# A gated attention unit followed by an FFT-convolution gate: output stores on three queues, a third tile between relu and square, and a planner that models two transfer queues

## The chip, the cores and the metric

The kernel runs on one core of one Trainium2 chip. The metric is the device time of one execution in microseconds, the median of several runs.

## The reference

Eight batches of 3136 rows. For each batch an attention without softmax (relu, then square), gated by `u`, and then a long convolution by FFT between two gates:

```python
scores = (1 / S) * z @ z.T                     # S = 3136, z is S x 64
x = u * (np.maximum(scores, 0) ** 2 @ v)       # u, v are S x 256
proj = x @ w_proj                              # 256 -> 3 * 256
x1, x2, x3 = proj[..., :D], proj[..., D:2*D], proj[..., 2*D:]
x2_conv = irfft(rfft(x2, axis=1) * rfft(filter_fft, axis=0), n=S, axis=1)
out = (x1 * x2_conv * x3) @ w_out              # float32, 8 x 3136 x 256
```

## The kernel before

The rows of a batch are cut into seven chunks of columns (`CHUNKS`: five of 512, one of 256, one of 320) and 25 tiles of 128 rows. For each chunk PE forms score tiles (`score_mm`, transposed, in the three pairs of PSUM banks `ps_s`). ACT applies relu into a tile `R`, ACT or DVE squares it into a tile `A` (`relu` L1819, `sq` L1826 and L1828), and PE multiplies by `v` (`weigh`, PSUM tiles `ps_o`). The scores are symmetric, so tiles for later chunks are transposed by DMA into `M1`, `M2e` and `M2o` instead of being computed twice (`mirror`, L1752). A score group of 64 contracted rows can also be issued as four 64x64 quadrants instead of two halves, which spares a change of PE's tiling next to transform work (the branch on `plan.mode`).

When a chunk of `x` is complete (`xT`, L1871), `add_proj` multiplies it by `w_proj`: the gates `x1 * x3` (`gate_t`, L1214) and the first stage of a two-stage transform (`dft1`, PE matmul `x_t,T`, tile `s_t`), which is stored to a DRAM scratch `spec_0` or `spec_1` (L1018). After all chunks `add_spectrum` loads this back in another layout (`load_spec`, L1048, four loads of three DMAs into `spec_in_t`), does the second stage on PE in 64x64 quadrants (`S`, tiles `xh` or `R`), multiplies by the filter's spectrum `H` (L1302), inverts it (`TZ`, tile `gs_t` and others) and stores it to scratch (L1347). `add_end` loads that by chunk (`load_c`, L1060, `conv_in_t`), does the last inverse stage (`T,conv_in_t`), multiplies by the gate (`yT_t`, L1388), multiplies by `w_out` (`wo,yT_t`), copies to a tile (`ost_t`) and stores it in `out` (L1447), two DMAs a chunk, one for each half of the partitions.

SP issues all plain transfers and DMA transposes, in one queue. POOL issues the loads that cast to 16 bit (`v_t`, `un_t`, `zn_t`, L649 and L668); each group of them waits for a `tick` (L658). In the last batch (b = 7) other tiles are free, so the spectrum's loads use `M_t` and `M2e_t` too, its stores come from `gs_t`, `M2o_t`, `A_t` and `uT_t`, and the loads of the inverse go to seven tiles `A_t`. Four chunks of batch 6 are held back (`HOLD = 3`, kind `FZ`) as work for the waits of the last batch; their results lie in `v_t` and `ost_t`. The last batch's own chunks end in the order of `FINAL`, with results in `R_t`, `xh` and `gs_t`.

The order of all of this is decided when the program is built. Every step is a `Task` with a cost on its engine, what it depends on and which buffers it takes. `Plan.go` replays the engines with these costs and emits the steps in the order in which it starts them. A step that moves data (`moves`) takes a place on a transfer bus: `moves` us after the one before it, no sooner than `DMA_GO` after its issue, landed `DMA_DONE` (and `late`) after that. Which kind of work PE takes next is a weighted sum over the plan's state (`pick_pe`); there are eight sets of weights, `a` to `h`, and the string `MIX` names one for every 12 steps. On the chip each engine follows this order, and semaphores hold it where the data are late.

Of the kernel before, what the change touches and what calls it, by code (L numbers as in the profile page):

```python
# [11 lines left out]
P = 128  # L12
F32 = mybir.dt.float32
BF16 = mybir.dt.bfloat16
# [4 lines left out]
N1 = 64  # L19
# [10 lines left out]
LATE_OUT = 2.0  # L30
AFTER = (1, 3, 5, 6)
# [7 lines left out]
class Weights:  # L39
# [82 lines left out]
    "chbeegbghbaageecebgfecfgbadeeedffbcgebdcgbececaahhfbceddhcdegbdhdhegdefcehbcagec"  # L122
    "abbbdgfdgbdhchhdchcaedhfhhaeacbaadeebfaaabfccdgdffdfaacccfebchccdabdfbdbeeccafae"
    "fhchhgabfghcchhgdfgdeggaaaa"
# [23 lines left out]
DMA_GO, DMA_DONE = 1.2, 0.8  # L148
# [121 lines left out]
class Plan:  # L270


    def __init__(self):
# [9 lines left out]
        self.bus = 0.0  # L283
# [31 lines left out]
    def run(self, task, engine, start):  # L315
# [130 lines left out]
def kernel(  # L446
# [57 lines left out]
    R_p = Pool("R", 2, [P, 2, 512], F32)  # L504
    A_p = Pool("A", 8, [P, 1024], BF16)
# [245 lines left out]
    filt_ld = [Task(lambda e, x=x: load_filter(*x), {"POOL": 1.6}, lat=10.0) for x in filt_cuts]  # L751
# [252 lines left out]
    def dft1(kind, get, t0, nt, dst, deps, free=None, late=0.0):  # L1004
# [20 lines left out]
        c = on("SP", put, 0.4, [b_], moves=0.35 * nt, late=late)  # L1025
# [16 lines left out]
    def load_spec(src, j0, nj, deps, late=0.0, home=l_p):  # L1042
# [7 lines left out]
        t = on("SP", go, 1.3, [*deps, *((d, ISSUED) for d in loads[-1:])], [home.slots], moves=0.6 * nj, late=late)  # L1050
        return in_order(t), box

    def load_c(src, c, deps, home):
# [8 lines left out]
        if home is c_p:  # L1062
            return in_order(on("SP", go, 0.45, [*deps, *((d, ISSUED) for d in loads[-1:])], [home.slots], moves=0.4 * nt, late=LATE_C)), box
        return on("SP", go, 0.45, deps, [home.slots], moves=0.4 * nt), box
# [203 lines left out]
    def add_spectrum(b, puts):  # L1268
# [9 lines left out]
        for g in range(NJ // 2):  # L1278
# [35 lines left out]
            def inv(g=g, xb=xb, z_=z_, a0=a0, gh=gh, mine=mine, per=per):  # L1314
# [29 lines left out]

                def put():
                    for rows, part in by_row(D2[b % 2], gx["g"], 2 * j0, 2 * per):
                        nc.sync.dma_start(out=rows, in_=part)  # L1347

                p_ = on("SP", put, 1.2, gx["es"], moves=0.5 * per, late=LATE_D2 * (not final))
# [10 lines left out]
    def add_end(b, lasts, gtasks, cs, kind="FB", src=c_p, dsts=(o_p,), late=0, behind=(), then=(), split=False, mids=(y_p,)):  # L1360
        for at, c in enumerate(cs):
# [82 lines left out]
            def store(i0, n, c=c, ob=ob):  # L1444
                r = rows_n1(out[b])
                for j, lo, hi, n2 in runs(T0[c] + i0, T0[c] + i0 + n):
                    nc.sync.dma_start(  # L1447
                        out=r[:, n2 : n2 + hi - lo, :], in_=ob["o"][ds(j * N1, N1), i0 : i0 + hi - lo, :]
                    )
# [515 lines left out]
```

## Time and profile before

| | us |
|---|---|
| timed runs | 992.66, 985.16, 992.11 |
| median | 992.11 |
| profiled execution | 981.7 |
| its span, first to last instruction | 979.9 |
| PE, ACT, DVE, POOL busy in the span | 940.6, 872.4, 827.4, 186.2 |
| DMA: moved in the span | 170.26 MB, mean 174 GB/s |

The profiled execution took 981.7 us, 10.4 less than the median of the timed runs. In rows of groups the columns are line, engine, operation, output from input with shapes, count, busy us, mean ns of one, and the idle time before them with what ended it. SPq is SP's instruction queue, in which DMAs are issued; the length of such a row is that of the issue, not of the transfer. Line numbers are those of the kernel before; in the rows of order of the changed kernel they are some 5 to 24 higher for the same statement.

### The profile page before, as it was taken

What the parts mean: (1) busy time and instruction counts of PE and PEld (TensorE: products, weight loads), DVE (VectorE), ACT (ScalarE), POOL (GpSimd) and SP (SyncE); (2) the same over time, 40 slices, a digit from 0 to 9 for tenths busy, and PEclk for the clock granted to TensorE, in tenths of its full rate; (3) what the DMA queues carried; (4) which work ended last, traced back from release to release, by engine and by line L of the source; (5) the groups of instructions that cost most, each with busy time, mean ns of one, the idle gap of its engine ahead of it and who ended that gap; (6) DMA issues with size and microseconds to landing.
All of it is one profiled execution on the core that took longest, in us unless ns stands there. A gap on an engine that the chain in (4) does not pass through costs nothing.

```text
span 979.9 us, 18879 instructions
## 1 busy us (share of the span) xinstructions
PE 940.6 (96%) x6450; PEld 468.4 (48%) x6560; DVE 827.4 (84%) x1449; ACT 872.4 (89%) x1203; POOL 186.2 (19%) x403
## 2 busy tenths in 40 slices
PE   6999999999999999999999999999999999999975
PEld 2343644355544554446544454445554365444644
DVE  7966788988889888888889978899889988799775
ACT  5996899999889899999989999899889999999774
POOL 5142311222021302113111320131102130001000
PEclk9999999999999999999999999999999999999989
DMA  9899688977999798998799878999699987995668
GB/s 163 139 165 174 115 175 165 180 141 138 188 208 199 155 184 168 189 184 154 152 222 194 170 151 169 206 175 178 145 191 213 185 149 168 199 179 129 170 175 244
DMA packets 332371, 170.26 MB, mean 174 GB/s; under 512 B 242442, under 2 KB 307786, under 8 KB 332276
## 3 DMA queue, kind: packets, MB, share of 16 engines
q1 hardware_dynamic: 304548, 138.10, 65.3%
q0 software_dynamic: 27728, 30.97, 23.6%
q8 instruction: 51, 0.84, 0.4%
q14 instruction: 44, 0.36, 0.1%
HBM read 90.26 MB, written 53.35 MB: 147 GB/s over the span
## 4 chain that ended last, share of the span: by engine, by line
PE 88%; DMA 4%; DVE 3%; ACT 2%; issue 1%; SPq 1%; ACTq 0%; DVEq 0%
PE ps_o_t L575 52%; PE ps_s L575 36%; DVE A_t L1828 1%; DMA spec_in_t<-spec 1%; DMA ost_t<-in_z_dram 1%; ACT R_t L1819 1%; DMA spec<-gs_t 1%; SPq L700 1%; DMA conv_in_t<-spec 1%; DMA spec<-s_t 0%; DMA A_t<-spec 0%; DVE yT_t L1388 0%; ACT xh L608 0%; ACT gs_t L608 0%; SPq L1447 0%
## 5 line engine op out<-in xcount | busy, mean ns | idle before, releaser
L1819 ACT ACTIVATE R_t<-ps_s 128x1024 f32<-128x1024 f32 (+4 forms) x512 | 473.7, 957 | 53.6 <-PE ps_s L575 39.3
L575 PE MATMUL ps_o_t<-A_t,v_t 128*128 128x512 bf16 (+3 forms) x1998 | 465.0, 354 | 8.0 <-issue 3.5
L1828 DVE TENSOR_TENSOR A_t<-R_t 128x1024 bf16<-128x1024 f32 (+3 forms) x312 | 346.1, 1128 | 77.6 <-ACT R_t L1819 76.9
L575 PEld LDWEIGHTS <-v_t 128*128 128x128 bf16 (+2 forms) x2846 | 249.8, 98 | 271.1 <-issue 88.4
L1826 ACT ACTIVATE A_t<-R_t 128x1024 bf16<-128x1024 f32 (+4 forms) x184 | 181.2, 990 | 2.1
L575 PE MATMUL ps_s<-zT_t 64*128 64x512 bf16 (+4 forms) x1246 | 152.5, 355 | 3.3 <-DVE s_t L612 2.0
L658 POOL COPY tick<-xT_t 1x1 bf16<-1x1 bf16 x54 | 11.7, 216 | 684.7 <-DVE xT_t L1871 669.4
L575 PE MATMUL ps_s<-xT_t,wp 128*128 128x512 bf16 (+2 forms) x392 | 105.0, 352 | 1.0 <-DVE gate_t L1214 0.4
L608 ACT ACTIVATE x_t<-ps_s 128x512 bf16<-128x512 f32 (+2 forms) x143 | 78.6, 565 | 10.7 <-PE ps_s L575 8.0
L1871 DVE SCALAR_TENSOR_TENSOR xT_t<-ps_o_t,uT_t 128x256 bf16<-128x256 f32 (+2 forms) x224 | 76.0, 380 | 13.3 <-PE ps_o_t L575 11.4
L575 PEld LDWEIGHTS <-zT_t 64*128 64x128 bf16 (+1 forms) x1279 | 49.9, 98 | 77.7 <-issue 60.1
L575 PE MATMUL ps_o_t<-M_t,v_t 128*128 128x512 bf16 (+2 forms) x352 | 81.9, 353 | 0.4
L1302 DVE TENSOR_TENSOR xh<-xh,H 128x1024 bf16<-128x1024 bf16 x120 | 81.3, 682 | 1.2 <-ACT xh L608 0.2
L1214 DVE TENSOR_TENSOR gate_t<-ps_s,x_t 128x256 bf16<-128x256 f32 (+2 forms) x214 | 72.8, 383 | 8.9 <-PE ps_s L575 5.3
L1388 DVE TENSOR_TENSOR yT_t<-ps_s,gate_t 128x512 bf16<-128x512 f32 (+2 forms) x99 | 59.3, 617 | 5.2 <-PE ps_s L575 3.7
L649 POOL DMA_DIRECT2D un_t<-in_u_dram x112 | 59.9, 556 | 9.4 <-issue 3.6
L668 POOL DMA_DIRECT2D v_t<-in_v_dram x112 | 59.5, 556 | 7.1 <-issue 3.1
L575 PE MATMUL ps_s<-wp,xT_t 128*128 128x256 bf16 x398 | 58.4, 273 | 0.2
L575 PEld LDWEIGHTS <-wp 128*128 128x128 bf16 x448 | 41.6, 98 | 34.4 <-issue 6.5
L608 ACT ACTIVATE xh<-ps_s 128x512 bf16<-128x512 f32 (+1 forms) x86 | 48.3, 607 | 8.8 <-PE ps_s L575 8.5
L575 PE MATMUL ps_s<-wo,yT_t 128*128 128x256 bf16 (+1 forms) x356 | 54.0, 273 | 0.4 <-DVE yT_t L1388 0.3
L608 ACT ACTIVATE s_t<-ps_s 128x512 bf16<-128x512 f32 x80 | 47.0, 592 | 2.3 <-PE ps_s L575 1.8
(149 smaller groups left out, 823.0 us busy)
## 6 DMA issues: line engine op xcount, KB each, us to landing
out_dram<-ost_t SPq DMA_DIRECT2D x66, 256.0 KB
spec<-s_t SPq DMA_DIRECT2D x96, 128.0 KB
spec_in_t<-spec SPq DMA_DIRECT2D x60, 192.0 KB
spec<-gs_t SPq DMA_DIRECT2D x60, 192.0 KB
v_t<-in_v_dram POOLq DMA_DIRECT2D x80, 128.0 KB, 5.0
un_t<-in_u_dram POOLq DMA_DIRECT2D x80, 128.0 KB, 5.2
conv_in_t<-spec SPq DMA_DIRECT2D x33, 256.0 KB
out_dram<-ost_t SPq DMA_DIRECT2D x19, 128.0 KB
```

Source lines behind the costliest of these rows:

```text
L575: wrote(nc.tensor.matmul(o, *args, **kw), o)
L608: got = nc.scalar.activation(out_, in_, AF.Copy)
L649: nc.gpsimd.dma_start(out=t[ds(j * N1, N1), lo - t0 : hi - t0, :], in_=x[:, n2 : n2 + hi - lo, :])
L658: nc.gpsimd.tensor_copy(tick[:], xt["t"][0:1, 1, 0:1])
L668: nc.gpsimd.dma_start(out=t[ds(j * N1, N1), ds(v_at(a), (b - a) * D)], in_=r[:, n2 + a - lo : n2 + b - lo, :].rearrange("p t d -> p (t d)"),)
L1214: got = nc.vector.tensor_tensor(g[:, ::-1] if h == 0 else g, p, x, ALU.mult)
L1302: nc.vector.tensor_tensor(x[:, 1 - i], x[:, 0], h, ALU.mult)
L1388: got = nc.vector.tensor_tensor(yb["y"][:, dh, 0:w], p, gates[b, c, dh][:, 0:w], ALU.mult)
L1819: has_read(nc.scalar.activation(blocks(box["R"], n, cw)[:rows], p, AF.Relu), p)
L1826: nc.scalar.activation(a, r, AF.Square)
L1828: nc.vector.tensor_tensor(a, r, r, ALU.mult)
L1871: nc.vector.scalar_tensor_tensor(x, f, inv_s2, ut, ALU.mult, ALU.mult)
```

## The change

1. *Stores.* In `add_end` a store names its queue. The last batch's chunks are stored half by SP and half by POOL, the last two of them half by SP and half by ACT; the last chunk's parts as before by pairs of tiles, of which it has one. The held chunks of batch 6 (kind `FZ`) are stored by POOL, both halves. In `add_spectrum` of the last batch the store of the last set but one (from `A_t`) goes to POOL. The stores of the second and third chunk of batch 6 that are not held have to be issued after the last first-stage store of the last batch (`put_off_stores`, joined with `puts[-1]`).
2. *Tiles.* `R` has three tiles instead of two, `A` seven instead of eight.
3. *The planner.* The bus becomes two, one for POOL and one for the others; when both are in use, each slows the other. The casting loads take a place on POOL's (0.515 us a tile) where they had a fixed 8 or 10 us. `DMA_GO` and `DMA_DONE` go from 1.2 and 0.8 to 0.9 and 0.6. The transfers' costs are set anew, those of the plain ones lower, those of the transposes mostly higher.
4. *The order.* `MIX` is another string of the same length; all weights stay.

```diff
-DMA_GO, DMA_DONE = 1.2, 0.8
+DMA_GO, DMA_DONE = 0.9, 0.6
...
-        self.bus = 0.0
+        self.bus = [0.0, 22.0]
...
         if task.moves:
-            self.bus = max(end + DMA_GO, self.bus) + task.moves
-            lat = self.bus + DMA_DONE + task.late - end
+            mine = int(engine == "POOL")
+            first = max(end + DMA_GO, self.bus[mine])
+            both = min(task.moves, max(0.0, self.bus[1 - mine] - first))
+            self.bus[mine] = first + task.moves + both
+            self.bus[1 - mine] += both
+            lat = self.bus[mine] + DMA_DONE + task.late - end
...
-    R_p = Pool("R", 2, [P, 2, 512], F32)
-    A_p = Pool("A", 8, [P, 1024], BF16)
+    R_p = Pool("R", 3, [P, 2, 512], F32)
+    A_p = Pool("A", 7, [P, 1024], BF16)
...
-        t = on("SP", go, 1.3, [*deps, *((d, ISSUED) for d in loads[-1:])], [home.slots], moves=0.6 * nj, late=late)
+        t = on("SP", go, 1.3, [*deps, *((d, ISSUED) for d in loads[-1:])], [home.slots], moves=0.37 * nj, late=late)
...
+                aside = final and mine == sets[-2]
...
-                        nc.sync.dma_start(out=rows, in_=part)
+                        (nc.gpsimd if aside else nc.sync).dma_start(out=rows, in_=part)
...
-            if split and c == cs[-1]:
-                for k, e_ in enumerate(oe):
-                    s_ = on("SP", lambda i0=2 * k, n=min(2, nt - 2 * k), store=store: store(i0, n), 0.9, [e_, *behind], prio=1, moves=0.9)
+            if split:
+                second = "ACT" if at >= len(cs) - 2 else "POOL"
+                parts = [(2 * k, min(2, nt - 2 * k), [e_]) for k, e_ in enumerate(oe)] if c == cs[-1] else [(0, nt, oe)]
+                todo = [
+                    (e, x, y, half, made_, 0.45 * y / 2) for x, y, made_ in parts for half, e in enumerate(("SP", second))
+                    if any(r_[0] == half for r_ in runs(T0[c] + x, T0[c] + x + y))
+                ]
             else:
-                s_ = on("SP", lambda nt=nt, store=store: store(0, nt), 1.3, [*oe, *behind], prio=1, moves=0.45 * nt, late=LATE_OUT * (dst is o_p))
-            s_.frees.append((o0, 1))
+                todo = [("POOL" if kind == "FZ" else "SP", 0, nt, None, oe, 0.45 * nt)]
...
+            if b == B - 2 and kind == "FB" and at:
+                put_off_stores.append(s_)
...
-                cu[slots[x]] = on("POOL", lambda: cast_u(*slots[x]), 1.1, [tick_], [un_p.slots], lat=8.0)
+                cu[slots[x]] = on("POOL", lambda: cast_u(*slots[x]), 1.1, [tick_], [un_p.slots], moves=CAST * len(tiles[slots[x][1]]), late=LATE_CAST)
...
+                        for t in put_off_stores:
+                            join(t, puts[-1], ISSUED)
```

How this moves instructions is shown at three places, each first as it was and then as it is.

DVE between the last cast of a first-stage tile `s_t` of the last batch and the first eviction of its spectrum, `xh_120`. In it `yT_t` is a product of the inverse with a gate (chunks of batch 6), `gate_t` a product of the last batch's projections. Before:

```order
L612 CAST s_t<-ps_s_139 128x256
L1214 TENSOR_TENSOR gate_t<-ps_o_t,x_t 128x4x64 x2
L1388 TENSOR_TENSOR yT_t<-ps_s_141,gate_t 128x512
L1388 TENSOR_TENSOR yT_t<-ps_s_139,gate_t 128x512
L1388 TENSOR_TENSOR yT_t<-ps_o_t,gate_t 128x512
L1214 TENSOR_TENSOR gate_t<-ps_s_141,x_t 128x4x64 x4
L1388 TENSOR_TENSOR yT_t<-ps_o_t,gate_t 128x512
L612 CAST xh_120<-ps_s_140 128x512
```

And after the change, the same stretch:

```order
L617 CAST s_t<-ps_s_139 128x256
L1395 TENSOR_TENSOR yT_t<-ps_s_140,gate_t 128x512
L1395 TENSOR_TENSOR yT_t<-ps_o_t,gate_t 128x512
L1219 TENSOR_TENSOR gate_t<-ps_s_140,x_t 128x4x64 x2
L1219 TENSOR_TENSOR gate_t<-ps_s_139,x_t 128x4x64 x2
L617 CAST xh_120<-ps_s_141 128x512
```

Two `yT_t` and two gate products have left this stretch; they stand behind the last multiplication by `H` now.

SP from the last stores of the last batch's spectrum to the loads of its inverse; `out_dram<-v_t` are stores of held chunks of batch 6. Before:

```order
L1347 DMA spec_1_62<-M2o_t 2x2048
L1347 DMA spec_1_62<-A_t 48x1024 x2
L1347 DMA spec_1_62<-A_t 2x1024
L1347 DMA spec_1_62<-uT_t 48x1024 x2
L1347 DMA spec_1_62<-uT_t 2x1024
L1447 DMA out_dram<-v_t 64x1024 x2
L1447 DMA out_dram<-v_t 64x512 x2
L1060 DMA A_t<-spec_1_62 128x4x256 x3
```

And now, where `ost_t` is a chunk of batch 6 that is not held:

```order
L1354 DMA spec_1_62<-M2o_t 2x2048
L1456 DMA out_dram<-ost_t 64x1024 x2
L1354 DMA spec_1_62<-uT_t 48x1024 x2
L1354 DMA spec_1_62<-uT_t 2x1024
L1065 DMA A_t<-spec_1_62 128x4x256 x3
```

The store from `A_t` and those of the held chunks have gone to POOL, and an output store stands ahead of the one from `uT_t`.

The end of SP's queue, the stores of the last batch's chunks. Before, both halves of each:

```order
L1447 DMA out_dram<-R_t 64x1024 x2
L1447 DMA out_dram<-xh_118 64x1024 x2
L1447 DMA out_dram<-gs_t 64x1024 x2
L1447 DMA out_dram<-R_t 64x768
L1447 DMA out_dram<-R_t 64x512
L1447 DMA out_dram<-xh_119 64x1024 x2
L1447 DMA out_dram<-gs_t 64x1024 x2
L1447 DMA out_dram<-xh_120 64x512 x2
```

After the change, SP's end:

```order
L1456 DMA out_dram<-R_t 64x1024
L1456 DMA out_dram<-xh_118 64x1024
L1456 DMA out_dram<-gs_t 64x1024
L1456 DMA out_dram<-xh_119 64x1024
L1456 DMA out_dram<-R_t 64x768
L1456 DMA out_dram<-gs_t 64x1024
L1456 DMA out_dram<-xh_120 64x512
```

And ACT's end, with its last three copies:

```order
L613 ACTIVATE R_t<-ps_o_t 128x512
L613 ACTIVATE R_t<-ps_o_t 64x256
L613 ACTIVATE xh_120<-ps_s_140 128x512
L1456 DMA out_dram<-gs_t 64x1024
L1456 DMA out_dram<-xh_120 64x512
```

Of each chunk one half has left SP; those of the last two chunks stand on ACT behind its last copy, the other five on POOL.

More of the change, by code (lines that the diff above doesn't have):

```diff
@@ L750 @@
     filt_cuts = ((0, 8), (8, 16), (16, NT))
[L751 removed]
+    filt_ld = [Task(lambda e, x=x: load_filter(*x), {"POOL": 1.6}, moves=CAST * (x[1] - x[0]), late=LATE_CAST) for x in filt_cuts]
     for x in filt_ld:
@@ L1555, in go_v @@
                     cv.setdefault(n, []).append(
-                        on("POOL", gv, 0.3 * (hi - lo), [tick_], [v_p.slots] if first else [], lat=8.0)
+                        on("POOL", gv, 0.3 * (hi - lo), [tick_], [v_p.slots] if first else [], moves=CAST * (hi - lo), late=LATE_CAST)
                     )
```

43 lines of the change are left out of this document (27 added, 16 removed).

## The prediction

> **What bounds the kernel now.** I read the page first, then the windows by stage, then the list of waits on PE, the chain of waits at the end, and the timeline of SP's queue there. The page, first span and busy time, then the chain and the groups used as prices:
>
> ```profile
> span 979.9 us, 18879 instructions
> PE 940.6 (96%) x6450; PEld 468.4 (48%) x6560; DVE 827.4 (84%) x1449; ACT 872.4 (89%) x1203; POOL 186.2 (19%) x403
> ...
> PE 88%; DMA 4%; DVE 3%; ACT 2%; issue 1%; SPq 1%; ACTq 0%; DVEq 0%
> ...
> L575 PE MATMUL ps_o_t<-A_t,v_t 128*128 128x512 bf16 (+3 forms) x1998 | 465.0, 354 | 8.0 <-issue 3.5
> ...
> L575 PE MATMUL ps_s<-wo,yT_t 128*128 128x256 bf16 (+1 forms) x356 | 54.0, 273 | 0.4 <-DVE yT_t L1388 0.3
> L575 PE MATMUL ps_s<-T,conv_in_t 128*128 128x128 bf16 (+1 forms) x324 | 30.5, 218 | 0.1
> ```
>
> TensorE is busy for 940.6 of 979.9 us, so only 39.3 us of the span are open to any change of order. Busy time over count gives prices: 465.0/1998 = 0.233 us for a 512-wide matmul, 54.0/356 = 0.152 for one of the output projection, 30.5/324 = 0.094 for one of the inverse transform. The windows say where the 39.3 us lie (busy time of PE, PEld, DVE, ACT, POOL, then clock, DMA share and GB/s):
>
> ```profile
> 0.00:14.00 14.00, 6.36 (x31) 2.43 (x31) 8.66 (x42) 6.56 (x10) 10.68 (x30) 1.00 0.86 169
> 14.00:75.00 61.00, 57.96 (x312) 24.06 (x318) 50.48 (x83) 54.22 (x67) 16.30 (x33) 1.00 0.98 152
> 75.00:82.00 7.00, 5.03 (x18) 1.49 (x14) 3.29 (x4) 3.25 (x4) 0.52 (x1) 0.76 1.33 132
> 82.00:925.60 843.60, 834.39 (x5713) 416.60 (x5814) 728.49 (x1247) 776.83 (x1064) 158.71 (x340) 1.00 0.90 174
> 925.60:934.30 8.70, 4.65 (x37) 2.71 (x35) 5.28 (x13) 3.31 (x6) 0.00 (x0) 1.00 0.55 146
> 934.30:950.10 15.80, 13.65 (x177) 8.15 (x180) 14.34 (x24) 13.62 (x28) 0.00 (x0) 0.78 0.59 162
> 950.10:971.90 21.80, 18.62 (x175) 12.93 (x175) 16.92 (x40) 14.64 (x29) 0.00 (x0) 1.00 0.84 248
> 971.90:979.90 8.00, 0.00 (x0) 0.00 (x0) 0.00 (x0) 0.01 (x1) 0.00 (x0) 0.72 0.64 210
> ```
>
> In the 843.6 us of the middle PE is busy for 834.4 (99%): nothing can be won there, only lost. The losses are 7.6 us in the first 14 (the first load, which the change leaves alone), 2 us at 75 to 82 with the clock at 0.76, and everything after 925.6: a wait of four us, a stretch of 21.8 us with PE at 18.62, and 8.0 us after the last copy in which no engine computes. PE's own waits, longest first:
>
> ```profile
> PE ps_s L578 <- ACT xT_t L608: 5.3, 1, 5.3
> PE ps_s L575 <- DMA spec_in_t<-spec: 5.0, 2, 4.1
> PE ps_o_t L575 <- issue: 3.5, 22, 0.2
> PE ps_s L575 <- DVE s_t L612: 2.0, 1, 2.0
> ```
>
> The spectrum's loads cost PE 5.0 us in two waits: 4.1 in the last batch, 0.9 in one earlier one. SP's queue at the end (start, length, what):
>
> ```profile
> 949.13 2.20 SPq L1347 DMA_DIRECT2D spec<-M2o_t  x3
> 951.44 1.80 SPq L1347 DMA_DIRECT2D spec<-A_t  x3
> 953.36 1.34 SPq L1347 DMA_DIRECT2D spec<-uT_t  x3
> 954.79 2.86 SPq L1447 DMA_DIRECT2D out_dram<-v_t  x4
> 957.76 4.23 SPq L1060 DMA_DIRECT2D A_t<-spec  x7
> ...
> 969.76 1.87 SPq L1447 DMA_DIRECT2D out_dram<-R_t  x2
> 971.72 1.20 SPq L1447 DMA_DIRECT2D out_dram<-xh  x2
> 973.02 1.86 SPq L1447 DMA_DIRECT2D out_dram<-gs_t  x2
> 974.97 1.78 SPq L1447 DMA_DIRECT2D out_dram<-xh  x2
> ```
>
> SP issues for 4.8 us after the last copy has ended (976.75 against 971.9), and the last bytes land 3.1 us later, at 979.9.
>
> **The change, part by part.** The sum is made against the profiled execution's own 981.7 us (span 979.9). The median of the three timed runs is 992.11, 10.4 us above; I carry the difference over to it.
>
> *Stores after the last copy.* Each chunk's store is now one half on SP and one on POOL (the last two chunks: on ACT). At 0.6 to 0.9 us a half (rows 971.72 to 974.97, two to a row) SP has one issue left after the last copy. ACT has two, since its half of the last chunk but one stands behind its own last copy; no issue on ACT is in the trace, so I price it by SP's rows, 1.2 to 1.8 for two, and take 1.5. Nothing else waits behind them. With 3.1 us to land that is 4.6 in place of 8.0, a gain of 3.4. The bounds: if nothing but the rate counts, 285 GB/s was moved while PE ended its work and 210 afterwards:
>
> ```profile
> 961.44:971.90 10.46, 9.30 (x100) 7.35 (x100) 8.00 (x15) 6.97 (x13) 0.00 (x0) 1.00 0.93 285
> ```
>
> That is 10.46 x 285 + 8.0 x 210 = 4.66 MB, or 16.4 us at 285 GB/s, which ends at 977.8: a gain of 2.1. Issue time alone gives 3.7 at most. I take the 3.4, because in the last stretch (next part) the data come later and so more slowly. The Trainium skill ("DMA: Bandwidth & Descriptors", section "Issuing engines are not separate DMA queues") says that transfers issued from several engines share the same 16 DMA engines, so that only issue time is saved; by it this part would be the 2.1 and not the 3.4. The trace leaves that open: a DMA share of 0.93 speaks for the rule, 0.64 after 971.9 against it.
>
> *Work moved behind the last spectrum.* The order rows of DVE show four yT products and six gate products between the last s_t cast and the first xh before, two and four now. On PE, 36 matmuls stood between the last first-stage transform and the first use of the spectrum, 16 now: four 512-wide, eight of the output and eight of the inverse fewer, 4 x 0.233 + 8 x 0.152 + 8 x 0.094 = 2.9 us of the 4.65 that covered the wait. The wait grows from 4.1 to about 7.0. That alone delays nothing: the chain through the transfers,
>
> ```profile
> 926.23 4.17 DMA spec<-s_t
> ...
> 931.30 2.98 DMA spec_in_t<-spec
> ...
> 957.76 3.63 DMA A_t<-spec
> ```
>
> keeps its length, since its stores stand in SP's queue as before, ahead of two of the four output stores that used to precede them. But the work comes back in the last stretch. After its last quadrant of the inverse, PE has eight more 512-wide, eight more output and twelve more inverse matmuls there: 8 x 0.233 + 8 x 0.152 + 12 x 0.094 = 4.2 us. DVE, after its last multiplication by H, has four more gate products, three more yT products and one more copy; by
>
> ```profile
> 955.21 1.62 DVE L1214 TENSOR_TENSOR gate_t<-ps_s,x_t 128x256 bf16<-128x256 f32 x4 [0.44 <-PE ps_s L575]
> 951.30 0.68 DVE L1388 TENSOR_TENSOR yT_t<-ps_o_t,gate_t 128x512 bf16<-128x512 f32 x1
> 950.70 0.69 DVE L612 CAST uT_t<-ps_s 128x512 bf16<-128x512 f32 x1
> ```
>
> that is 1.62 + 3 x 0.68 + 0.69 = 4.4 us. PE then needs 18.62 + 4.2 = 22.8 us in a stretch of 21.8, DVE 16.92 + 4.4 = 21.3. So the last copy comes at least 1.0 later; with the idle 3.2 us of before less the 0.7 that PE waited for A_t, 3.5 later. I take 2.2, midway.
>
> *The held stores and one spectrum store to POOL.* SP loses the 1.80 of spec<-A_t and the 2.86 of out_dram<-v_t ahead of the A_t loads. These can start up to 1.9 us sooner, but PE has work for that time now (above), so I cost it at nothing; without that cover it is worth the 0.7. POOL has nothing else to do after 925.6 (0.00 busy), so nobody waits behind these issues; a POOL issue costs about 0.56, as in the casts.
>
> *Third R tile, seven A tiles.* ACT's relu no longer waits for the square two before it; in the middle PE is at 99%, so this hides behind PE: nothing, and the lost A tile the same.
>
> *New order, new transfer costs.* PE's work is the same, but for 156 half-size score matmuls that became 78 whole ones. It changes its tiling 607 times instead of 601; the gaps at such a place are
>
> ```profile
> 883.44 0.05 issue
> ...
> 908.68 0.16 issue
> ```
>
> so six more cost 0.3 to 1.0, I take 0.6. Between the last first-stage transform of a batch and the first use of its spectrum stood at least 89 matmuls before; now 76 and 82 in batches 3 and 4. The planner counts shorter transfers, so I allow one more wait of the earlier kind, 0.9 (5.0 - 4.1); below it nothing, above it one in each of the seven earlier batches and at as many loads behind them, about 8. In the head one transpose held SP for 6.94 us against a median of 1.26 (minimum, median, maximum in ns):
>
> ```profile
> L1752 SPq DMA_TRANSPOSE M_t<-A_t x96: 1159/1260/6937, 16.6 to 908.7; - x96
> ```
>
> It ended in PE's wait of 2.0 for s_t, then half a clock for some 3.5 us. The rows around it stand otherwise now, and 95 of 96 such transposes were shorter, so I count the 2.0 as won; between 0 (it comes again) and 3.7 (the clock too).
>
> Sum: -3.4 + 2.2 + 0.6 + 0.9 - 2.0 = -1.7 us: 981.7 becomes 980.0, and on the median 992.11 becomes 990.4.
>
> **Rivals.** *The transfers take it back, no gain at the end.* If the stores after the last copy are bound by rate, they start later by the 2.2 and gain only 2.1: the end gives +0.1. With the stall of the head coming again and 1.5 in the middle the time is 993.7. For it speaks the DMA share of 0.93 in the stretch that now holds more work; against it the falling rate after 971.9.
>
> *Slower: the planner's shorter transfers.* With first uses set closer to their loads, PE stands still in the middle. Place: the first use of the spectrum and of its second to fourth loads. Price: 0.9 to 4.1 a wait (the two seen). From two waits of 2.5 (midway) it outweighs all gains; with four, and the stall of the head in its place, the time is 992.11 - 3.4 + 2.2 + 0.6 + 10 = 1001.5. For it: 76 and 82 against 89. Against it: batch 0 and 2 had 91 and 89 before, and no wait.
>
> *Faster: the order hides more.* The head gains 3.7, the last stretch grows by 1.0 only, six tilings cost 0.3, and the 9.2 us of idle between 82 and 925.6 shrink by half: -3.4 + 1.0 + 0.3 - 3.7 - 4.6 = -10.4, or 981.7. For it: the third R tile and transfers counted where the casts run. Against it: most of these 9.2 us are short gaps of issue.
>
> *The change doesn't do what it says* (issues wait on POOL or ACT as on SP) falls together with the first rival.
>
> **How the numbers follow.** A measurement of this kernel can tell about 1% from no change (the three runs lie 0.8% apart). The forecast (-6 to +1, so 986 to 993) has 0.42, no gain 0.22, slower 0.20, faster 0.16. Faster by over 1% is the last alone, 0.16; within 1% the first two, 0.64; slower 0.20. The range holds the forecast, the case of no gain and about half of each of the others: down to 978, which is the faster case less half of the 0.8% that the runs lie apart, and up to 1001, the slower case; what lies beyond is about 0.1 on the slow side and 0.05 on the fast one.
>
> **What would show it.** Right: after the last copy 4 to 5 us, not 8; two engines' stores side by side; the wait for spec_in_t near 7 and the last stretch 23 to 25 us; DVE and PE there above 90%. Wrong: 7 us or more after the last copy (first rival), waits of PE for spec_in_t or conv_in_t in batches 3 and 4 (second), or a transpose of some 7 us again near 75. A middle whose idle time is under 5 us would make the forecast too slow.

## The result, and the profile after

| | before | after |
|---|---|---|
| median, us (20 runs each, one disturbed run of 1097.75 after left out of the comparison) | 987.68 | 986.82 |
| lowest and highest of the others | 979.83 to 992.66 | 984.07 to 990.87 |
| ratio after/before, 95% interval | | 0.9998 [0.9977, 1.0018] |
| profiled execution, its span | 981.7, 979.9 | 984.44, 982.7 |

The change makes no difference that these runs can tell. The median of before over 20 runs is 4.4 us below the 992.11 of the three runs shown first, and its profiled execution is among its shortest. So the two profiles differ by more (+2.8 us in span) than the medians (-0.9), and single stages are compared below over several runs.

The page of after, first its span and PE, then the chain that ended last:

```profile
span 982.7 us, 18875 instructions
...
PE 950.0 (97%) x6484; PEld 467.6 (48%) x6484; DVE 809.5 (82%) x1426; ACT 873.3 (89%) x1226; POOL 199.3 (20%) x419
...
PE 89%; DMA 5%; DVE 2%; SPq 1%; ACT 1%; issue 1%; DVEq 0%; ACTq 0%
```

PE shows 9.4 us more than before. Most of that is no new work: before, the trace has 6560 weight loads and 6450 matmuls, so some 110 matmul records are missing; now both are 6484. Idle time of PE that was read from the profile before is therefore too long in places. The windows of after, cut at the same events as those of before (last cast of `s_t`, first use of the spectrum, last quadrant of the inverse, last copy), with the same columns:

```profile
82.00:925.44 843.44, 839.82 (x5726) 415.25 (x5725) 709.93 (x1219) 776.13 (x1086) 163.05 (x339) 1.00 0.89 174
925.44:932.35 6.91, 1.71 (x9) 0.59 (x7) 2.61 (x6) 1.20 (x3) 0.00 (x0) 0.83 0.84 230
932.35:948.55 16.20, 14.80 (x185) 7.50 (x186) 13.48 (x23) 13.58 (x28) 0.00 (x0) 0.75 0.41 107
948.55:974.16 25.61, 21.49 (x192) 14.93 (x192) 19.96 (x47) 16.54 (x32) 8.57 (x16) 1.00 0.89 260
974.16:982.67 8.51, 0.00 (x0) 0.00 (x0) 0.00 (x0) 0.00 (x0) 0.00 (x0) 0.72 0.44 138
```

To set beside these, the same events of before to 0.01 us are 926.66, 934.32, 950.60, 971.91 and the end 979.90. The last `s_t` is 1.2 sooner, the wait for the spectrum 0.75 shorter (6.91 against 7.66), the last stretch 4.3 longer (25.61 against 21.31), and the time behind the last copy is not shorter: 8.51 against 7.99. PE's waits of after, longest first:

```profile
PE ps_s L580 <- DMA spec_in_t<-spec: 6.6, 2, 5.2
PE ps_s L583 <- ACT xT_t L613: 5.5, 1, 5.5
PE ps_s L580 <- DMA A_t<-spec: 2.3, 2, 1.6
...
PE ps_s L580 <- DVE s_t L617: 1.1, 1, 1.1
```

The wait for the last spectrum is 5.2; all others for `spec_in_t` are 1.4 together (6.6 - 5.2). The waits for `A_t<-spec` are 2.3, where there was one of 0.7 before.

What ended the program stands in POOL's queue. The rows of its drain, an instruction that the program has at its end on each engine, of after and then of before (minimum, median and maximum in ns, first and last start):

```profile
L1984 POOLq DRAIN  x3: 46/102/8721, 973.2 to 982.4; - x3
```

```profile
L1960 POOLq DRAIN  x3: 45/102/7487, 904.0 to 979.6; - x3
```

Before, POOL's last issue was at 904.0, and its drain of 7.49 us was over at 911.5. After the change POOL issues its last half store at 973.19, the drain starts there and takes 8.72 us, to 981.88; 0.8 later the program ends. SP reaches its own drain rows when its last transfers have landed:

```profile
L1984 SPq DRAIN  x3: 7/7/13, 979.6 to 982.1; - x3
```

That is at 979.6, 2.3 us before POOL's drain is over; in before SP was there at 979.1, 0.8 before the end. The windows say the same: no byte starts to move in the last 3.8 us of after (0 GB/s from 978.90 to 982.67), against 1.5 us in before (978.40 to 979.90). The ends of SP's queue and of POOL's, in after:

```profile
973.42 0.47 SPq L1456 DMA_DIRECT2D out_dram<-R_t  x1
973.98 0.55 SPq L1456 DMA_DIRECT2D out_dram<-gs_t  x1
974.62 1.21 SPq L1456 DMA_DIRECT2D out_dram<-xh  x1
```

```profile
971.33 0.54 POOL L1456 DMA_DIRECT2D out_dram<-xh  x1 [1.79 <-ACT xh L613]
973.19 0.54 POOL L1456 DMA_DIRECT2D out_dram<-R_t  x1 [1.32 <-ACT R_t L613]
```

SP is done with its issues 1.7 us after the last copy (975.83 against 974.16; before 4.85), so the split did at SP what was forecast. The transfer itself isn't what the drain lasts for: POOL's last store had landed 3.7 us after its issue, near 976.9, by the list of DMA issues:

```profile
out_dram<-R_t POOLq DMA_DIRECT2D x1, 128.0 KB, 3.7
```

### The profile page after: what moved, and what is told of

Its sections match the earlier page's. It is cut to its first block, busy times and chain, and to the rows that moved or that the text cites. A ratio compares the mean times of both kernels' runs of the same rounds, so it can differ in the third digit from the quotient of the medians.

```text
span 982.7 us, 18875 instructions
## 1 busy us (share of the span) xinstructions
PE 950.0 (97%) x6484; PEld 467.6 (48%) x6484; DVE 809.5 (82%) x1426; ACT 873.3 (89%) x1226; POOL 199.3 (20%) x419
## 4 chain that ended last, share of the span: by engine, by line
PE 89%; DMA 5%; DVE 2%; SPq 1%; ACT 1%; issue 1%; DVEq 0%; ACTq 0%
PE ps_o_t L580 53%; PE ps_s L580 36%; DMA M_t<-A_t 2%; DMA spec_in_t<-spec 1%; DMA A_t<-spec 1%; DMA M2e_t<-A_t 1%; DMA ost_t<-in_z_dram 1%; DVE A_t L1850 1%; SPq L705 1%; ACT x_t L613 0%; SPq L1053 0%; DMA spec<-uT_t 0%; DVE R_t L1307 0%; DVE uT_t L1395 0%; DVE xT_t L617 0%
## 5 line engine op out<-in xcount | busy, mean ns | idle before, releaser
L1841 ACT ACTIVATE R_t<-ps_s 128x1024 f32<-128x1024 f32 (+4 forms) x512 | 463.8, 967 | 47.8 <-PE ps_s L580 43.7
L580 PE MATMUL ps_o_t<-A_t,v_t 128*128 128x512 bf16 (+4 forms) x2074 | 475.9, 355 | 1.7 <-DVE A_t L1850 1.6
L1850 DVE TENSOR_TENSOR A_t<-R_t 128x1024 bf16<-128x1024 f32 (+3 forms) x306 | 338.9, 1125 | 80.1 <-ACT R_t L1841 72.3
L1848 ACT ACTIVATE A_t<-R_t 128x1024 bf16<-128x1024 f32 (+4 forms) x190 | 190.5, 1010 | 3.6 <-DMA M_t<-A_t 2.3
L663 POOL COPY tick<-xT_t 1x1 bf16<-1x1 bf16 x54 | 16.0, 296 | 679.8 <-DVE xT_t L1893 679.8
L580 PE MATMUL ps_s<-zT_t 64*128 64x512 bf16 (+4 forms) x1168 | 149.5, 356 | 1.0 <-DVE zT_t L617 0.5
L580 PE MATMUL ps_s<-xT_t,wp 128*128 128x512 bf16 (+2 forms) x434 | 112.3, 352 | 1.4 <-DVE s_t L617 1.1
L613 ACT ACTIVATE x_t<-ps_s 128x512 bf16<-128x512 f32 (+2 forms) x149 | 82.1, 579 | 13.0 <-PE ps_s L580 11.1
L613 ACT ACTIVATE s_t<-ps_s 128x512 bf16<-128x512 f32 (+1 forms) x83 | 48.7, 602 | 7.3 <-PE ps_s L580 5.7
L580 PE MATMUL ps_s<-wo,yT_t 128*128 128x256 bf16 (+1 forms) x340 | 51.4, 273 | 0.0
```

The source lines that it names most:

```text
L580: wrote(nc.tensor.matmul(o, *args, **kw), o)
L613: got = nc.scalar.activation(out_, in_, AF.Copy)
L663: nc.gpsimd.tensor_copy(tick[:], xt["t"][0:1, 1, 0:1])
L1841: has_read(nc.scalar.activation(blocks(box["R"], n, cw)[:rows], p, AF.Relu), p)
L1848: nc.scalar.activation(a, r, AF.Square)
L1850: nc.vector.tensor_tensor(a, r, r, ALU.mult)
```

## The experiments

Three theories of the time behind the last copy: *issue* (the one on record: SP's queue sets it), *rate* (the first rival: the bytes left and what 16 DMA engines move), and *drain* (formed from the profile of after: POOL's drain sets it, if POOL issues late). For the last stretch, from the last quadrant of the inverse to the last copy: the moved work alone, or the held stores that now run beside the loads of `A_t`. Ratios are to the kernel before in the same call, with 95% intervals. All kernels keep the order that their planner gave; only the queue or the place of an issue is edited, except in `before_r3`. Stages are read from one profile of each kernel.

**halves_act.** After, with POOL's halves of the last batch on ACT.

```diff
-                queue = {"SP": nc.sync, "ACT": nc.scalar, "POOL": nc.gpsimd}[e]
+                queue = {"SP": nc.sync, "ACT": nc.scalar, "POOL": nc.scalar if b == B - 1 else nc.gpsimd}[e]
```

> The changed kernel, but the five half stores of the last batch that went to POOL are issued by ACT; the planner still counts them as POOL's, so the order on PE, DVE and SP is the same. Drain theory: the end of the program waits for POOL's drain, which lasts until about 8 us after POOL's last DMA issue (8.7 us from 973.2 in the changed kernel, 7.5 us from 904.0 in the one before). POOL's last issue is then the one of the held chunk near 959, so the drain is over long before, and the end is set by the last landing on SP and ACT: the span falls from 982.7 to about 980.5, and POOL's long drain ends near 967. Rate theory: the last stores are bound by how fast the bytes move, whichever queue issues them: the span stays at 982.7 within 0.5. Cost that both allow: five issues of 0.5 us on ACT among its copies, up to 1 us.

984.56 us, 0.9975 [0.9948, 1.0002]. POOL's drain was over at 972.95, the program ended at 986.28, 6.55 us after the last copy. But the last copy came 51.3 us after the last `s_t`, 2.6 later than in after. I first took this for ACT's issues, four of which (0.56, 0.51, 0.50, 0.50) now lie among its copies, and the expectation of `order_act2` below says so. PE's waits behind 945 show another reason for a part of it:

```profile
PE ps_s L580 <- DMA A_t<-spec: 3.3, 3, 1.9
PE ps_o_t L580 <- ACT x_t L613: 0.4, 1, 0.4
```

PE waited 3.3 us for the loads of `A_t` here (2.3 in after), and in `both`, below, the same seven issues on ACT delay nothing that can be seen. This explains 1.0 of the 2.6; the rest stays open, and the profile of this kernel (988.12) is long beside its median.

**held_behind.** After, with the held stores on SP behind the last load of `A_t`.

```diff
+                last_loads.append(c)
+                if len(last_loads) == NC:
+                    loads_out.append(True)
+                    for x in waiting_stores:
+                        x()
...
-                queue = {"SP": nc.sync, "ACT": nc.scalar, "POOL": nc.gpsimd}[e]
+                if kind == "FZ" and not loads_out:
+                    waiting_stores.append(lambda: store(e, i0, n, half, c, ob))
+                    return
+                queue = {"SP": nc.sync, "ACT": nc.scalar, "POOL": nc.sync if kind == "FZ" else nc.gpsimd}[e]
```

> The changed kernel, but the held chunks' stores of batch 6 go to SP, behind the seven loads of A_t, instead of to POOL beside them. Contention theory: these 1.8 MB moved side by side with the loads and stretched the first one from 3.6 to 7.4 us; without them the loads land by about 959.5 instead of 962.5, PE's waits of 2.3 us for A_t go, and the last copy comes about 2 us sooner, near 972; since POOL's last issue moves with it, the span falls to about 980.7. Rival, the cover theory: PE, ACT and DVE have work until 962 anyway, so the last copy moves by less than 0.7 us and the span stays between 982 and 983.5.

984.06 us, 0.9980 [0.9958, 1.0001]. From the last quadrant of the inverse to the last copy 23.54 us, 2.1 less than in after. In the waits of PE behind 925 none for `A_t` is left:

```profile
PE ps_s L580 <- DMA spec_in_t<-spec: 5.1, 1, 5.1
PE ps_s L580 <- ACT xh L613: 0.6, 1, 0.6
PE ps_o_t L580 <- DVE yT_t L1402: 0.6, 1, 0.6
```

So about half of the 4.3 by which the stretch grew goes with the wait for `A_t`, and comes from held stores that move before the loads are through. (The five kernels with the order of before and both tiles as before have 21.0 to 23.3 us there, so a single profile is good to a microsecond or two; `both`, with 23.3, repeats the result.) The end was still POOL's: its drain from 974.25 to 982.91, the program to 984.13, 8.89 after the last copy.

**both.** The two edits together.

> Both edits together: the held chunks' stores on SP behind the loads of A_t, the five halves of the last batch on ACT. Drain and contention theory: 2.2 and 2.0 us add, the span is about 978.5, the ratio to the kernel before about 0.996. Drain theory alone: 980.5. Rate and cover theory: 982.7.

985.52 us, 0.9996 [0.9974, 1.0019]. The last copy came 45.9 us after the last `s_t`, as soon as before (45.25), with the halves on ACT and no wait for `A_t`, but the end 10.39 later. The eight held issues kept SP busy until 971, and their bytes were still to be moved. The window from the last copy to the end:

```profile
973.16:983.55 10.39, 0.00 (x0) 0.00 (x0) 0.00 (x0) 0.00 (x1) 0.00 (x0) 0.61 0.74 216
```

That is 216 GB/s x 10.39 us = 2.24 MB, against 1.17 in after. What was won in the stretch was paid behind it.

**order_only.** After, with every store on SP as before.

```diff
-                queue = {"SP": nc.sync, "ACT": nc.scalar, "POOL": nc.gpsimd}[e]
+                queue = nc.sync
...
-                        (nc.gpsimd if aside else nc.sync).dma_start(out=rows, in_=part)
+                        nc.sync.dma_start(out=rows, in_=part)
```

> The changed kernel's order, tiles and planner, but every store is issued by SP as in the kernel before; the order on PE and DVE is the same as in the changed one. The prediction's price of the split stores (a gain of 3.4 at the end) would make this 3.4 us slower than the changed kernel, a span of about 986. Drain theory: here nothing waits for POOL; the last copy comes at about 974, SP needs some 8 us from there as before, span about 982, the same as the changed kernel within 1: the split won about 3 us at the landing and the drain took it away.

984.46 us, 0.9979 [0.9952, 1.0007]. Without any split the end came 6.68 us after the last copy: sooner than with it (8.51), and sooner than before (7.99), although SP's last issue was 3.4 us after the last copy. Last `s_t` to last copy: 48.3.

**late_pool and early_pool.** Before, with one half store on POOL: that of the last chunk, or that of the first (`FINAL[0]` for `FINAL[-1]`).

```diff
-                    nc.sync.dma_start(
+                    (nc.gpsimd if split and c == FINAL[-1] and j else nc.sync).dma_start(
```

> The kernel before, with one half of the very last store (the 64 x 512 of xh) issued by POOL instead of SP; all else in the same order. Drain theory: POOL issues it right after the last copy (971.9 to 972.5), its drain lasts until about 8 us after that, so the program ends about 9.5 us after the last copy instead of 8.0, although SP has one issue of 1.1 us less: span about 981.5. Rate theory, or no theory of POOL: one issue less on SP ends the program 0 to 1.1 us sooner: span 978.8 to 980.

> The kernel before, with one half of the last batch's first chunk (the first R_t, issued near 965) on POOL instead of SP. Drain theory: the drain is over near 974, before the last landing; the end is SP's, with one issue of 0.6 us less in its queue: 7.4 to 8.0 us after the last copy, span 979.3 to 980. If it is not the lateness but any use of POOL in the tail that costs, the program ends as late as with the late half on POOL, 9.5 us after the last copy.

987.69 us, 1.0010 [0.9982, 1.0038], and 987.59 us, 1.0006 [0.9977, 1.0035]; what they tell is in their profiles. POOL's drain in the first and in the second:

```profile
L1960 POOLq DRAIN  x3: 51/93/7703, 977.9 to 986.1; - x3
```

```profile
L1960 POOLq DRAIN  x3: 51/102/7488, 968.9 to 982.8; - x3
```

Each has one half store on POOL. Issued 0.3 us after the last copy, its drain ends at 985.63 and the program 0.8 later, 8.75 after the last copy. Issued 6.5 us before the last copy, the drain ends at 976.35, 6.8 before the program does, and the end comes 7.71 after the last copy. A single late issue on POOL is enough to let its drain end the program; here it costs 0.8 us against before (7.99).

**stores_only.** Before, with the queues of the change.

```diff
+                    queue = nc.sync
+                    if split and j:
+                        queue = nc.scalar if c in FINAL[-2:] else nc.gpsimd
+                    if kind == "FZ":
+                        queue = nc.gpsimd
...
-                        nc.sync.dma_start(out=rows, in_=part)
+                        (nc.gpsimd if final and mine == sets[-2] else nc.sync).dma_start(out=rows, in_=part)
```

> The order, tiles and planner of the kernel before, with the queues of the change for every store (held chunks and the A_t spectrum on POOL, halves of the last batch on POOL and for the last two chunks on ACT). The prediction's price: 4.6 us from the last copy to the end instead of 8.0, nothing elsewhere, span 976.5. Drain theory: POOL's last issue stands near 970, its drain ends near 978, and the end comes about 7 us after the last copy, span about 979. Contention beside it: the held stores run beside the loads of A_t, the first of them takes 5 us or more instead of 3.6, and the last copy comes up to 1 us later.

986.83 us, 1.0014 [0.9987, 1.0042]. SP's last issue ended 2.0 us after the last copy, POOL's drain at 981.59 (9.34 long), the program 8.86 after the last copy. The stores alone bring no difference that can be told.

**before_r3.** Before, with three tiles `R` and seven `A`, in the order that was planned for two and eight.

```diff
-    R_p = Pool("R", 2, [P, 2, 512], F32)
-    A_p = Pool("A", 8, [P, 1024], BF16)
+    R_p, A_p = Pool("R", 3, [P, 2, 512], F32), Pool("A", 7, [P, 1024], BF16)
+    R_p.slots, A_p.slots = Slots(2), Slots(8)
```

> The order of the kernel before (its planner still counts two R tiles and eight A tiles), but the buffers themselves are three and seven, as in the change. The prediction costs the third R tile and the lost A tile at nothing, since PE is busy throughout the middle: last first-stage tile of the last batch at 926.7 within 1.5 as before, last copy and end as before, ratio within 0.2% of 1. If the third tile frees ACT in the head, where ACT and DVE set the pace until 29 us, that tile comes up to 1.5 us sooner; if seven A tiles hold back the squares while transposes still read them, up to 3 us later.

993.67 us, 1.0080 [1.0049, 1.0112], the only kernel that is clearly off. The tiles without an order made for them cost 0.8%:

```profile
PE ps_s L575 <- DMA spec_in_t<-spec: 7.5, 3, 3.8
PE ps_s L575 <- DVE s_t L612: 4.8, 1, 4.8
...
PE ps_o_t L575 <- DVE A_t L1828: 3.6, 4, 2.4
```

Each of the three was shorter in before (5.0, 2.0, 1.5); in the first 110 us alone PE does 4.3 us less (92.77 busy against 97.08). The last `s_t` ends at 939.6, 13 us later than in before. But the wait for `s_t`, and of the waits for `spec_in_t` the one ahead of the last batch (2.2), are within what the other kernels with this order show (up to 5.7 and 3.9), so these rows don't name the cause. Nor does the run tell the third `R` from the lost `A`: the two weren't tried apart.

**before_act2.** Before, with only the second halves of the last two chunks on ACT.

```diff
-                    nc.sync.dma_start(
+                    (nc.scalar if split and j and c in FINAL[-2:] else nc.sync).dma_start(
```

> The order and the queues of the kernel before; only the second halves of the last two chunks are issued by ACT. If issue time on SP sets the end (before: SP's last issue ended 4.85 us after the last copy, the program 7.99 after it), SP is left with about 2.5 us of issues behind the last copy and the program ends about 6 us after it: 2 us faster, 985.3 where before is 987.3. If the rate of the transfers sets the end, it stays at 8.0 and the ratio at 1.000. POOL issues nothing late in either case, so its drain ends near 912 and plays no part.

988.09 us, 1.0017 [0.9987, 1.0047], the end 8.34 after the last copy: no gain. SP's end in this kernel, and the longest of its waits there:

```profile
982.16 0.84 SPq L1447 DMA_DIRECT2D out_dram<-gs_t  x1
986.72 0.47 SPq L1447 DMA_DIRECT2D out_dram<-xh  x1
```

```profile
SPq L1447 <- DMA out_dram<-gs_t: 3.7, 1, 3.7
```

SP stood for 3.7 us before its last issue, with the data there since 981.8. The semaphores in the trace tell why: the transfers that SP and ACT issue are counted on eight semaphores (100 to 107) in turn, over both engines, and an issue waits until the transfer that had its semaphore before has landed. SP's last store has number 103, and so had ACT's `gs_t` half, issued 5 us before. So this run doesn't tell issue from rate by itself.

**order_act2.** `order_only` with the second halves of the last two chunks on ACT (`nc.scalar if e == "ACT" else nc.sync`).

> The order of the changed kernel, no output or spectrum store on POOL, the second halves of the last two chunks on ACT. With all stores on SP this order ended 6.68 us after its last copy. Issue theory: 5.0 to 5.5 us after the last copy, so about 1.3 us less than with SP alone (ratio about 0.997). Rate theory: 6.7 again. If ACT's two issues delay copies, as they did where ACT had seven of them (last copy 2.6 later), the last stretch grows from 48.3 by 0.5 at most.

984.42 us, 0.9974 [0.9954, 0.9995], the best ratio of all and the only one whose interval leaves out 1 on the fast side. That is one of twelve intervals and by a hair, and the medians of the same call, 984.42 and 985.52, are 0.1% apart, so a gain on before isn't shown. The end came 6.83 after the last copy, as with SP alone (6.68); SP's last store again waited for the semaphore of ACT's, 1.3 us. That is what the rate theory expected, though this wait blurs it.

**held_pool_act2.** After, with POOL's halves back on SP; the held stores and the spectrum store stay on POOL.

```diff
-                queue = {"SP": nc.sync, "ACT": nc.scalar, "POOL": nc.gpsimd}[e]
+                queue = nc.scalar if e == "ACT" else nc.gpsimd if kind == "FZ" else nc.sync
```

> The changed kernel with the halves that it gave to POOL back on SP; the held chunks and the one spectrum store stay on POOL, whose last issue then comes near 959. Drain theory: POOL's drain ends near 967 and no longer ends the program, so that the end comes about 5.5 us after the last copy in place of 8.51: 3 us faster than the changed kernel. Rate theory: 8 us or more, as in the changed kernel, since the same bytes move at the same time.

985.46 us, 0.9992 [0.9971, 1.0014]. POOL's drain, 10.37 long, ended at 971.04, and the end came 6.88 after the last copy: 1.6 less than in after with the same order, not the 3.0 expected of the drain alone. Neither theory has the number by itself: when the drain is gone, about the time by rate is left (6.5 in the table below). The whole program gained less, because the last copy came 50.2 us after the last `s_t` (48.7 in after).

**pool_three.** Meant to leave POOL the halves of the first three chunks (`e == "POOL" and (kind == "FZ" or at <= 2)`).

> The changed kernel, but only the first three chunks have a half on POOL (its last issue near 969.5 in place of 973.7); the fourth and fifth chunk go to SP whole, the last two stay on SP and ACT. Drain theory: the drain ends 8 to 9 us after the last issue, near 978, about 4 us sooner than in the changed kernel, so that SP and ACT end the program 5 to 6 us after the last copy, which is 2.5 to 3 us faster than the changed kernel and the best of these. Rate theory: no difference from the changed kernel, 8 us or more after the last copy.

985.85 us, 0.9994 [0.9972, 1.0016]. The condition is evaluated when the store is emitted, and `at` is then that of the last chunk, so no half went to POOL. It is `held_pool_act2` once more, and repeats it: 7.03 from the last copy to the end (6.88), 49.6 from the last `s_t` to the last copy (50.2). These differences of 0.15 and 0.6 are between two profiles of one program. What was asked stays untried.

**All of them at the end.** Bytes moved after the last copy (GB/s of the window from there to the end, times its length), by 0.28 MB per us, plus 2.2 us, against the measured end. The 0.28 is about the mean of the first 4 us after the last copy, which is 255 to 303 GB/s in all 14 kernels; the 2.2 is fitted to the upper nine.

| kernel | MB | MB/0.28 + 2.2 | measured | last issue of SP or ACT after the last copy |
|---|---|---|---|---|
| before | 1.67 | 8.2 | 7.99 | 4.9 |
| before_r3 | 1.68 | 8.2 | 8.13 | 4.9 |
| early_pool | 1.65 | 8.1 | 7.71 | 4.4 |
| order_only | 1.31 | 6.9 | 6.68 | 3.4 |
| order_act2 | 1.30 | 6.8 | 6.83 | 3.9 |
| pool_three | 1.24 | 6.6 | 7.03 | 2.9 |
| held_pool_act2 | 1.21 | 6.5 | 6.88 | 2.8 |
| halves_act | 1.15 | 6.3 | 6.55 | 1.9 |
| both | 2.24 | 10.2 | 10.39 | 6.1 |
| after (drain) | 1.17 | 6.4 | 8.51 | 1.7 |
| late_pool (drain) | 1.68 | 8.2 | 8.75 | 4.4 |
| stores_only (drain) | 1.43 | 7.3 | 8.86 | 2.0 |
| held_behind (drain) | 1.67 | 8.2 | 8.89 | 3.4 |
| before_act2 (semaphore) | 1.52 | 7.6 | 8.34 | 5.4 |

In the upper nine the rate holds to 0.4 us. The last issue does not: in `halves_act` it comes 1.5 us sooner than in `order_only`, and the end 0.1 sooner. Only rows six to nine decide this: in the first five, and in `before_act2`, the last issue plus 2.9 to 3.3 us would fit as well, while these four would need over 4. Whether issues or bytes end before itself is therefore not settled; shown is that in the new order sooner issues don't bring the end sooner. In the four marked (drain) the end lies 0.6 to 2.1 above the rate, and in each 0.8 to 1.2 us behind the end of POOL's drain. The first 4 us after the last copy, with one queue (before) and with three (after), show the rate; the last two columns are DMA share and GB/s:

```profile
971.91:975.91 4.00, 0.00 (x0) 0.00 (x0) 0.00 (x0) 0.00 (x1) 0.00 (x0) 0.94 0.83 271
```

```profile
974.16:978.16 4.00, 0.00 (x0) 0.00 (x0) 0.00 (x0) 0.00 (x0) 0.00 (x0) 0.96 0.90 284
```

The rule of the Trainium skill weighed in the prediction ("DMA: Bandwidth & Descriptors", section "Issuing engines are not separate DMA queues": all issuers share the 16 engines) agrees with these rows: three queues move hardly more than one, 284 against 271 GB/s.

## Why the prediction was right, and which of its steps were wrong

The forecast of no measurable change came true, and 986.82 lies in the range. The steps it was made of were only partly right, and their errors cancelled: the end and the last stretch came out some 5 us worse than forecast (+0.5 for -3.4, +3.5 for +2.2), and what lies ahead of the last `s_t` some 3 better (about -3.4 for -0.5, over several profiles). That the sum was near is luck in good part.

*Stores after the last copy, -3.4: wrong, +0.5 measured.* The failing sentence is "I take the 3.4, because in the last stretch the data come later and so more slowly". The issues were as forecast, over 1.7 us after the last copy (1.5 forecast). What failed is the "3.1 us to land" behind them: it is 4.6 in `halves_act`, where no drain counts, and 6.8 in after. Fewer bytes were left (1.17 MB for 1.67), worth (1.67 - 1.17)/0.28 = 1.8 us by rate, near the 2.1 that the prediction had as the bound from the rate and gave up; most of it is the order's, since `order_only`, with all stores on SP, has 1.31 MB left. On top came POOL's drain, 2.1 above the rate in after, which took all of it. The drain was to be seen in the trace of before, 7.49 us behind POOL's last issue at 904.0, and I didn't ask what a late issue on POOL would move it to. "POOL has nothing else to do after 925.6, so nobody waits behind these issues" was the oversight: the program's end waits. The rival "the transfers take it back, no gain at the end" named the right result at this place (+0.1 forecast); its time of 993.7 was too high for the reasons below.

*Last stretch, +2.2: the direction right, the size too small by about the wait for A_t.* It grew by 4.3; 0.75 came back in the shorter wait ahead of it, so from the last `s_t` to the last copy it is +3.5 (48.7 against 45.25), and +3.1 with `order_only`. `held_behind` splits the stretch: 2.1 of the 4.3 goes with the wait for `A_t`, and 2.2 is left for the moved work, as forecast. PE's busy time there grew by 3.4 (18.12 to 21.49, for 4.2 forecast). The other runs stand in the same order. From the last `s_t` to the last copy the order of before took 45.3 to 46.1 us (before, `late_pool`, `early_pool`, `stores_only`, `before_act2`), the new order 45.9 and 46.8 with the held stores behind the loads, 48.3 twice with them on SP ahead of and between the loads, and 48.7 to 51.3 in the four kernels with them on POOL beside the loads. Most of the growth is the order: `order_only` has 3.1 of the 3.5 already, with a wait of 1.7 for `A_t`. The queue adds 0.4 there, and 1.3 to 1.9 between `order_act2` (48.3) and `held_pool_act2` and `pool_three` (50.2, 49.6), which differ from it in nothing but the held stores and one spectrum store on POOL. In the order of before the queue does little: in `stores_only` POOL's last six held issues (955.3 to 959.4) are nearly over when the loads begin (958.4), PE waits 1.0 for `A_t`, and the time is 45.7; in after all eight run from 952.8 to 959.1, and the loads from 954.6. PE and DVE are 84% and 78% busy there (21.49 and 19.96 of 25.61), not above 90%; without the wait, in `held_behind`, PE is at 92% (21.57 of 23.53).

*Held stores to POOL, nothing: too low, by the 0.4 to 1.9 us above.* The loads of `A_t` were issued sooner, as forecast (by 3.1 us, 954.62 against 957.76; I had said up to 1.9), but PE could use the first of them only 0.5 sooner (960.91 against 961.44), and the second not at all sooner (962.52 against 962.21). The chain of after:

```profile
928.83 3.47 DMA spec_in_t<-spec
...
951.73 2.69 DMA spec<-uT_t
955.04 7.43 DMA A_t<-spec
```

The first load, issued at 954.62, was there for PE 6.3 us later, in before 3.7 us after its issue; the second, in this chain, took 7.43. The "cover" of which the prediction spoke was there and was too short: PE waited 2.3 in place of 0.7. Taking an issue out of a queue had been counted, and not that its bytes then share the engines with what follows.

*Wait for the spectrum, from 4.1 to 7.0: 5.2.* The cover shrank as forecast, but the time from the last `s_t` to the first use of the spectrum got 0.75 shorter too. That the chain "keeps its length" was wrong by this much in these two profiles; over all it is 6.3 to 7.9 us in the order of before and 6.7 to 6.9 in the new one. Why was not tried.

*Head and middle, -2.0 + 0.6 + 0.9 = -0.5: right in sign, too small.* The head's wait for `s_t` is 1.1 in after instead of 2.0 (its longest transpose, at 73.5, took 5.11 us, where one at 72.9 took 6.94), and no waits came in batches 3 and 4, so the slower rival did not occur (one wait of 1.4 us for another spectrum, against 0.9). The idle time of the middle, which was to be a sign above or below 5 us, fell from 9.2 to 3.6, but the middle is hardly shorter (843.44 us against 844.66 to the last `s_t`): much of the 9.2 must be missing matmul records, and the sign told nothing. The time of the last `s_t` varies from run to run: over the profiles in the order of before 926.7, 932.1, 930.1, 927.8 and 935.7 (mean 930.5), in the new order 925.1 to 928.4 in eight (mean 927.1). So the new order reaches that point some 3.4 us sooner (standard error 1.7 by these spreads) and more evenly. That would pay for the longer end; the narrower range of whole times (984 to 991 against 980 to 993) says the same. The traces show where it comes from. In the order of before PE waits for `s_t` near 80 us and for a spectrum near 280 us; the two add up to 2.9, 6.8, 5.4, 3.8 and 9.6 us in these five profiles, and less them the last `s_t` lies within 923.8 to 926.1 in all five. In the new order the same kinds of wait ahead of the last batch add up to 0 to 2.5 us, 1.7 in the mean against 5.7. So the 0.9 that the prediction priced a wait for the spectrum at was the lowest of 0.9 to 3.9 (up to 1.5 in the new order): instead of one more wait there was less waiting. Which edit of the planner brings it was not tried.

*Third R and lost A tile, nothing: not shown.* `before_r3` lost 0.8% with them in the old order; in the new one they were not tried apart from it, and the whole kernel shows no loss.

The absolute forecast of 990.4 lies 3.6 above the result, because it was carried over to a median of three runs that lay 4.4 above the median of 20.

## What to carry to other kernels

Before a store is given to another queue, ask whether the issues or the bytes end last: the DMA share and GB/s of the first microseconds after the last computation help to tell (0.83 and 271 with one queue here, 0.90 and 284 with three). Look in GpSimd's queue for a drain behind its last transfer, and count it to the program's end if that transfer is late: in the four kernels here that issue on it within 1 us of the last copy, the end came 0.8 to 1.2 us after the drain. Look at several profiles before a wait is given a price: one seen as 0.9 was up to 3.9 in others. A store that is taken from ahead of a load on one queue, and put beside it on another, still shared the engines with it here (load there 6.3 us after its issue in place of 3.7).

## What the hardware showed that I had not expected

- POOL's drain after its last DMA issue is 7.49 to 11.14 us long in the runs here: 7.49 to 8.67 where the last issue came before 917, 7.49 and 7.70 behind one half store, 8.66 to 9.34 behind the halves of the last batch (`held_behind`, after, `stores_only`), 9.16 behind the spectrum's store (`both`), 9.46 to 11.14 where the held stores were its last issues (`pool_three`, `held_pool_act2`, `halves_act`). In after it ended 5 us later than its last transfer. What sets its length is not settled.
- Eight semaphores serve the transfers of SP and ACT together in these programs, so a short queue can stand behind the other engine's transfer: 3.7 us in `before_act2`, 1.3 in `order_act2`.
- The first two `A_t` loads took 6.3 and 7.4 us beside stores, the first 3.7 when those went ahead in the same queue; the window of the last stretch shows 260 GB/s at a DMA share of 0.89 in after.
